# A one-token decoder block in float32: the ring of load buffers moved to a multiple of 256 bytes, and two late weight loads each cut in two

## The chip, the cores and the metric

The kernel runs on one core of a Trainium2 chip. The metric is the device time of one execution in microseconds (us), the median of several runs. The profile and the trace are those of one further execution, whose span is the time between the first and the last recorded instruction.

## The reference

One decode step of a block with adaptive layer norm, two batch rows, everything in float32. Attention looks at the last W = 4096 of 32768 cached positions.

```python
# B=2, D=512, HQ=32 query heads, HKV=8 key/value heads, DH=128, F=1792
mod = (silu(c) @ w_mod).reshape(2, 6, 1, 512)          # sa, ca, ga, sb, cb, gb
h = layernorm(x) * (1 + ca) + sa
q = (h @ wq) split into 32 heads
p = softmax(q . k_cache[:, :, -4096:] * 128**-0.5)      # 4 query heads share one k/v head
x = x + ga * ((p @ v_cache[:, :, -4096:]) @ wo)
h = layernorm(x) * (1 + cb) + sb
x = x + gb * (silu(h @ w1) @ w2)                        # w1 512x1792, w2 1792x512
```

## The kernel before

All of the large inputs come from device memory through one queue, SyncE's, into one ring: the pool `ring` of RING = 8 buffers, each 4096 floats (16,384 bytes) on each of 128 partitions. 45 loads stand in the queue in the order of the program and take the ring's buffers in turn: `w_mod` in four (`wm`), `wq` in four, then for each of 16 pairs t of key/value head and batch row one load of keys (`load_k`) and one of values (`load_v`), `wo` in four (`wo0`, `wo8`, `wo16`, `wo24`), `w1` in two (`w1_0`, `w1_2`), `w2` in four (`w2_0`, `w2_8`, `w2_11`, `w2_13`). The last ten are made by `load_runs`; the number in a name is the first row per partition that the load holds. A load may start when its ring buffer has been released by the engine that read what stood in it last, and when the load eight before it has landed. Some loads of a few kilobytes (`c_ch`, `x_ch`, `x_sp`) go to the pool `consts`, and so does every small constant that is built on the chip.

What one partition reads in one piece differs: 12,288 bytes of `w_mod`, 16,384 of `wq`, of the keys and of `wo`, four pieces of 4,096 for the values, 14,336 for each half of `w1`.

Work on a pair t: VectorE transposes the keys block by block (L341), TensorE multiplies them with the queries (L359), maximum and exponent follow on VectorE, TensorE and ScalarE, and TensorE weighs the values of the pair before (L303). After the last pair comes a tail in which each step needs the one before it:

- `acc_o` and `ao` (L475, L484): the attention output times `wo`, eight rows per partition from each of the four loads.
- layer norm: `x1T`, `mean_b`, `hT_b` on VectorE and TensorE.
- `hid` (L516): `hT_b` times `w1` in four steps k = 0..3; k = 0, 1 read `w1_0`, k = 2, 3 read `w1_2`. Between k = 1 and k = 2 stands the small product `var_b` (L525).
- `hidT`, `z`, `sgh`, `uT` (L533 to L545): transpose and SiLU on VectorE and ScalarE.
- `acc_yw` (L549): `uT` times the first eight rows per partition of `w2` (all in `w2_0`), tt = 0..7; then `acc_y` (L559) for tt = 8..13, with `gather` (L462) bringing `acc_yw` in after tt = 10.
- `yo` (L569, L570) and the store of the output (L572), also in SyncE's queue.

No scheduler reorders this: each engine runs its instructions in the order in which the program writes them. A matmul of the program is two records in the trace.

The pools are laid out in each partition one after the other in the order in which the function opens them. In the kernel before `consts` is opened first, and the ring begins at byte 49,088 of each partition, which is 192 above a multiple of 256. All eight buffers, 16,384 bytes apart, begin 192 above a multiple of 256.

Of the kernel before, what the change touches and what calls it, by code (L numbers as in the profile page):

```python
# [8 lines left out]
F32 = mybir.dt.float32  # L9
# [4 lines left out]
P = 128  # L14
# [5 lines left out]
RING = 8  # L20
# [3 lines left out]
def adaln_block(  # L24
# [24 lines left out]
    SCALE = DH**-0.5  # L49
    assert W == 4096  # L50

    consts = ctx.enter_context(tc.tile_pool(name="consts", bufs=1))
    ring = ctx.enter_context(tc.tile_pool(name="ring", bufs=RING))
    ktp = ctx.enter_context(tc.tile_pool(name="ktp", bufs=2))
    work = ctx.enter_context(tc.tile_pool(name="work", bufs=2))
    once = ctx.enter_context(tc.tile_pool(name="once", bufs=1))
# [3 lines left out]
    def const(shape, name):  # L60
        return consts.tile(shape, F32, name=name)

    def bank(tag, name):
        return (psum1 if tag in "CO" else psum).tile([P, 512], F32, tag=tag, name=name)

    def stream(name):
        return ring.tile([P, 4096], F32, tag="st", name=name)
# [20 lines left out]
    def load_runs(name, w, per, lo, hi):  # L88

        e = w.shape[1]  # L90
        t = stream(f"{name}{lo}")[:, : (hi - lo) * e].rearrange("p (q e) -> p q e", e=e)
        nc.sync.dma_start(t, w.rearrange("(p q) e -> p q e", q=per)[:, lo:hi, :])
        return t
# [19 lines left out]
    ident = const([P, P], "ident")  # L113
    make_identity(nc, ident)

    id4 = const([P, 32], "id4")
    nc.vector.tensor_reduce(
        id4, ident.rearrange("p (a r) -> p r a", r=32), axis=AX.X, op=ALU.add
    )
# [300 lines left out]
    ax = once.tile([P, P], F32, tag="ax", name="ax")  # L420
    for q0 in range(0, 32, 8):
        wot.append(load_runs("wo", wo, 32, q0, q0 + 8))
    w1t = [load_runs("w1_", w1, 4, k, k + 2) for k in (0, 2)]
    T2, WIDE = F // P, 8
    w2t = {}
    for lo, hi in ((0, WIDE), (WIDE, 11), (11, 13), (13, T2)):
        wt = load_runs("w2_", w2, T2, lo, hi)
        for tt in range(lo, hi):
            w2t[tt] = wt[:, tt - lo, :]
# [43 lines left out]
    for q in range(24):  # L473
        g = q % 4
# [37 lines left out]
    FC = F // 4  # L512
    hp = bank("A", "hid")[:, :FC]
    for k in range(4):
        for g in range(4):
            nc.tensor.matmul(  # L516
                hp[32 * g : 32 * g + 32, :],
                hT[:, k, :],
                w1t[k // 2][:, k % 2, g * FC : (g + 1) * FC],
                start=(k == 0),  # L520
                stop=(k == 3),
            )
        if k == 1:
            var = bank("B", "var_b")
            nc.tensor.matmul(var[:, :B], mean512, vs, start=True, stop=True)  # L525
            std = once.tile([P, B], F32, tag="stdb", name="std_b")
            nc.scalar.activation(std, var[:, :B], AF.Sqrt, bias=eps_t)
            rstd = once.tile([P, B], F32, tag="rstdb", name="rstd_b")
            nc.vector.reciprocal(rstd, std)
# [17 lines left out]
    for tt in range(WIDE):  # L547
        g = tt % 4
# [51 lines left out]
```

## Time and profile before

| what | value |
|---|---|
| median of 3 runs | 245.63 us (245.63 to 245.86) |
| the profiled execution | 245.34 us |
| its span | 243.1 us |
| TensorE busy | 154.8 us (64%) |
| VectorE busy | 102.4 us (42%) |
| ScalarE busy | 34.9 us (14%) |
| moved by DMA | 97.82 MB in 13467 packets |
| mean granted TensorE clock | 0.823 |

A busy share is an average over the whole span. Which engine or transfer sets the end is read from the chain that ended last and from the waits in each stage. The profiled execution took 2.24 us more than its span, which is what lies around the first and the last recorded instruction.

### The profile page before, as it was taken

To read this page: it belongs to the slowest core of one execution; us is meant where nothing else is said; L and a number is where in the kernel's file an instruction comes from. 1 tells how busy PE (TensorE), PEld (TensorE's weight loads), DVE (VectorE), ACT (ScalarE), POOL (GpSimd) and SP (SyncE) were. 2 spreads that over 40 slices of the span, in tenths; PEclk is the share of its full clock that TensorE was granted. 3 is DMA by queue.
4 is the path that set the end of the run, shared out by engine and by line. 5 is a ranking of instruction groups with operands and counts; after the bars stand their busy time and mean duration, and the time that the engine had idled before them with its cause. 6 is when DMAs were issued, how large, how long until landed. Compare 5 with 4: busy or idle time off the path is not lost.

```text
span 243.1 us, 4593 instructions
## 1 busy us (share of the span) xinstructions
PE 154.8 (64%) x2040; PEld 82.7 (34%) x2040; DVE 102.4 (42%) x179; ACT 34.9 (14%) x96; POOL 7.4 (3%) x27
## 2 busy tenths in 40 slices
PE   0294656067786596692963948487396488864854
PEld 0221001023453463451642625255163256103213
DVE  0604003772754835726457263563736721002030
ACT  2300000103320211220102112021111202003200
POOL 8000000000000000000000000000000000000000
PEclk9999579655997978897699789679869979779577
DMA  7999999999999999999999999999999999999970
GB/s 257 422 434 431 431 426 426 408 431 401 427 421 405 433 400 426 421 406 434 399 429 419 404 432 402 431 415 408 431 404 419 403 431 429 426 428 429 420 295 1
DMA packets 13467, 97.82 MB, mean 402 GB/s; under 512 B 888, under 2 KB 904, under 8 KB 9480
## 3 DMA queue, kind: packets, MB, share of 16 engines
q1 hardware_dynamic: 13448, 97.54, 97.0%
q8 instruction: 16, 0.26, 0.4%
q14 instruction: 3, 0.02, 0.0%
HBM read 97.53 MB, written 0.00 MB: 401 GB/s over the span
## 4 chain that ended last, share of the span: by engine, by line
DMA 67%; DVE 16%; PE 14%; SPq 1%; issue 1%; ACT 0%; POOL 0%; DVEq 0%; POOLq 0%
DMA k<-in_A_k_cache_dram 38%; DMA w<-in_B_w_dram 14%; DVE kT L341 12%; DMA wq<-in_A_wq_dram 12%; PE s L359 8%; DMA c_ch<-in_c_dram 2%; PE hid L516 1%; PE acc_yw L549 1%; PE o L303 1%; PE acc_y L559 1%; DVE qT L270 1%; SPq L71 1%; PE q L261 0%; DVE qbd L284 0%; DVE mx L367 0%
## 5 line engine op out<-in xcount | busy, mean ns | idle before, releaser
L359 PE MATMUL s<-kT,qbd 128*32 128x256 f32 x512 | 48.2, 532 | 49.0 <-DVE kT L341 49.0
L341 DVE STREAM_TRANSPOSE kT<-k 128x1024 f32<-128x1024 f32 x64 | 73.9, 1207 | 9.4 <-DMA k<-in_A_k_cache_dram 9.4
L303 PE MATMUL o<-v,ptb 128*32 128x128 f32 x1024 | 45.5, 297 | 0.0
L359 PEld LDWEIGHTS s<-kT,qbd 128*32 128x32 f32 x512 | 19.6, 145 | 70.0 <-DVE kT L341 53.4
L303 PEld LDWEIGHTS o<-v,ptb 128*32 128x32 f32 x1024 | 36.0, 119 | 5.6 <-issue 3.1
L367 DVE TENSOR_REDUCE mx<-s 128x1 f32<-128x256 f32 x16 | 6.8, 425 | 48.3 <-PE s L359 48.3
L391 ACT COPY bias<-bp 128x1 f32<-128x1 f32 x16 | 2.6, 160 | 123.2 <-PE bp L389 123.2
L261 PE MATMUL q<-wq,hq_T 128*32 128x512 f32 x64 | 11.7, 869 | 9.7 <-DMA wq<-in_A_wq_dram 9.7
L393 ACT ACTIVATE pr<-s,bias 128x256 f32<-128x256 f32 x16 | 11.8, 741 | 0.5
L475 PE MATMUL acc_o<-wo,oTn 128*32 128x512 f32 x48 | 8.6, 851 | 3.4 <-DMA wo<-in_A_wo_dram 3.1
L270 DVE STREAM_TRANSPOSE qT<-q 128x512 f32<-128x512 f32 x2 | 1.4, 717 | 19.1 <-PE q L261 18.8
L261 PEld LDWEIGHTS q<-wq,hq_T 128*32 128x32 f32 x64 | 2.2, 137 | 19.2 <-DMA wq<-in_A_wq_dram 11.1
L369 PE MATMUL mT<-ident,mx 128*1 128x128 f32 x32 | 7.3, 316 | 1.1 <-DVE mx L367 1.1
L375 DVE TENSOR_REDUCE mg<-mT 1x4 f32<-1x64 f32 x16 | 3.4, 210 | 10.5 <-PE mT L369 10.5
L406 PE MATMUL pT<-ident,pr 128*128 128x128 f32 x32 | 7.0, 300 | 0.4
L516 PE MATMUL hid<-w,hT_b 128*32 128x448 f32 x32 | 5.8, 868 | 1.8 <-DMA w<-in_B_w_dram 1.2
L494 DVE STREAM_TRANSPOSE aoT<-ao 128x128 f32<-128x128 f32 x1 | 0.3, 317 | 15.4 <-PE ao L484 15.4
L389 PEld LDWEIGHTS bp<-negscale,mrow 1*128 1x128 f32 x32 | 4.9, 190 | 5.6 <-DVE mrow L381 4.8
L409 ACT COPY ptb<-pT 128x256 f32<-128x256 f32 x16 | 6.0, 372 | 5.4 <-PE pT L406 5.3
L317 PE MATMUL o_all<-ob,selh 128*32 128x128 f32 x32 | 6.5, 284 | 0.4 <-ACT ob L312 0.4
L389 PE MATMUL bp<-negscale,mrow 1*128 1x1 f32 x32 | 6.2, 262 | 0.7 <-DVE mrow L381 0.2
L193 PE MATMUL mean_a<-mv_a,avg 128*128 128x1 f32 x2 | 0.6, 363 | 8.8 <-DVE mv_a L190 8.8
(123 smaller groups left out, 88.6 us busy)
## 6 DMA issues: line engine op xcount, KB each, us to landing
k<-in_A_k_cache_dram SPq DMA_DIRECT2D x16, 2048.0 KB, 32.0
v<-in_A_v_cache_dram SPq DMA_DIRECT2D x16, 2048.0 KB, 27.7
wq<-in_A_wq_dram SPq DMA_DIRECT2D x4, 2048.0 KB
wo<-in_A_wo_dram SPq DMA_DIRECT2D x4, 2048.0 KB, 27.9
wm<-in_w_mod_dram SPq DMA_DIRECT2D x4, 1536.0 KB, 8.6
w<-in_B_w_dram SPq DMA_DIRECT2D x2, 1792.0 KB
w<-in_B_w_dram SPq DMA_DIRECT2D x1, 2048.0 KB
w<-in_B_w_dram SPq DMA_DIRECT2D x1, 768.0 KB
```

What stands on the lines that cost most here:

```text
L261: nc.tensor.matmul(q_ps[n][32 * g : 32 * g + 32, :], hq_T[:, k, :], wv[:, n, g], start=(k == 0), stop=(k == 3),)
L303: nc.tensor.matmul(o_ps[32 * i : 32 * i + 32, :], pt[:, n % 2, o : o + 32], vt[:, i, n, :], start=(n == 0), stop=(n == 7),)
L317: nc.tensor.matmul(o_all[:, b, :], selh[:, HQ - G - G * h : 2 * HQ - G - G * h], weighted.o_sb, start=(t == 0), stop=(t == NP - 1), skip_g ...
L341: nc.vector.transpose(kT[t][:, n4].rearrange("p n j r -> p (n j r)"), kt[t][:, n4 * 1024 : (n4 + 1) * 1024],)
L359: nc.tensor.matmul(s_ps[32 * cc : 32 * cc + 32, :], qbd[h // 4][:, h % 4, b, j, :], kT[t][:, :, 2 * cc : 2 * cc + 2, j, :], start=(j == 0) ...
L367: nc.vector.tensor_reduce(mx, s_ps, axis=AX.X, op=ALU.max)
L369: nc.tensor.matmul(mT[0:1, :P], mx, ident, start=True, stop=True)
L389: nc.tensor.matmul(bp[:, 0:1], m, negscale, start=True, stop=True)
L393: nc.scalar.activation(pr.rearrange("p s k n -> p n s k"), s_ps.rearrange("p (n s k) -> p n s k", n=4, s=2), AF.Exp, bias=bias, scale=SCAL ...
L406: nc.tensor.transpose(tp[:, s * P : (s + 1) * P], pr[:, s].rearrange("p k n -> p (k n)"), ident)
L475: nc.tensor.matmul(acc[32 * g : 32 * g + 32, :], oTn[:, q, :], wot[q // 8][:, q % 8, :], start=(q < 4), stop=(q >= 20),)
L516: nc.tensor.matmul(hp[32 * g : 32 * g + 32, :], hT[:, k, :], w1t[k // 2][:, k % 2, g * FC : (g + 1) * FC], start=(k == 0), stop=(k == 3),)
```

## The change

The function opens a new pool `head` first, which holds the constant `id4` (128 bytes), and then the ring, before `consts`. With `id4` in front the ring begins at byte 16,640, which is 65 times 256. `consts` lies behind the ring and has the same size less `id4`. The loads of `w1` become three (`w1_0` as before, then one row per partition each in `w1_2` and `w1_3`, 7,168 bytes a piece), and the first eight rows of `w2` come in two loads of four (`w2_0`, `w2_4`, 8,192 bytes a piece).

```diff
+    head = ctx.enter_context(tc.tile_pool(name="head", bufs=1))
+    id4 = head.tile([P, 32], F32, name="id4")
+    ring = ctx.enter_context(tc.tile_pool(name="ring", bufs=RING))
     consts = ctx.enter_context(tc.tile_pool(name="consts", bufs=1))
-    ring = ctx.enter_context(tc.tile_pool(name="ring", bufs=RING))
...
-    id4 = const([P, 32], "id4")
...
-    w1t = [load_runs("w1_", w1, 4, k, k + 2) for k in (0, 2)]
+    w1t = []
+    for lo, hi in ((0, 2), (2, 3), (3, 4)):
+        wt = load_runs("w1_", w1, 4, lo, hi)
+        w1t.extend(wt[:, k, :] for k in range(hi - lo))
...
-    for lo, hi in ((0, WIDE), (WIDE, 11), (11, 13), (13, T2)):
+    for lo, hi in ((0, 4), (4, WIDE), (WIDE, 11), (11, 13), (13, T2)):
...
-                w1t[k // 2][:, k % 2, g * FC : (g + 1) * FC],
+                w1t[k][:, g * FC : (g + 1) * FC],
```

SyncE's queue at its end, from the first load of `w1` on. The shapes are partitions by floats; behind a row stand the semaphores it waits for, `DMAHW` for the landing of an earlier load, PE or DVE for the engine that releases the ring buffer. Before:

```order
L92 DMA w1_0_1570<-in_B_w1_dram 128x3584 [waits DMAHW1_49,PE_49]
L92 DMA w1_2_1572<-in_B_w1_dram 128x3584 [waits DMAHW2_49,DVE_49]
L92 DMA w2_0_1574<-in_B_w2_dram 128x4096 [waits DMAHW3_49,PE_49]
L92 DMA w2_8_1576<-in_B_w2_dram 128x1536 [waits DMAHW4_49,PE_49]
L92 DMA w2_11_1578<-in_B_w2_dram 128x1024 [waits DMAHW5_49,PE_49]
L92 DMA w2_13_1580<-in_B_w2_dram 128x512 [waits DMAHW6_49,PE_49]
L572 DMA out_0_dram<-yo_1754 4x2x128 [waits DMAHW7_49,DVE_49]
```

The same place in the queue after the change:

```order
L95 DMA w1_0_1573<-in_B_w1_dram 128x3584 [waits DMAHW1_49,PE_49]
L95 DMA w1_2_1575<-in_B_w1_dram 128x1792 [waits DMAHW2_49,DVE_49]
L95 DMA w1_3_1577<-in_B_w1_dram 128x1792 [waits DMAHW3_49,PE_49]
L95 DMA w2_0_1579<-in_B_w2_dram 128x2048 [waits DMAHW4_49,PE_49]
L95 DMA w2_4_1581<-in_B_w2_dram 128x2048 [waits DMAHW5_49,PE_49]
L95 DMA w2_8_1583<-in_B_w2_dram 128x1536 [waits DMAHW6_49,PE_49]
L95 DMA w2_11_1585<-in_B_w2_dram 128x1024 [waits DMAHW7_49,PE_49]
L95 DMA w2_13_1587<-in_B_w2_dram 128x512 [waits DMAHW0_49,PE_49]
L577 DMA out_0_dram<-yo_1761 4x2x128 [waits DMAHW1_49,DVE_49]
```

Two loads more, and each load from `w1_3` on takes a later buffer of the ring and a later semaphore. Before, `w2_11` and `w2_13` took the buffers of `wo0` and `wo8`. Now `w2_4` and `w2_8` take those, and `w2_11` and `w2_13` take the buffers of `wo16` and `wo24`.

TensorE's queue in the tail, from the first product with `w1` on (a count behind a row is the number of matmuls in a line). Before:

```order
L516 MATMUL hid_1678<-w1_0_1570,hT_b_225 32x448 x8
L525 MATMUL var_b_1687<-vs_1676,mean512_126 128x2
L516 MATMUL hid_1678<-w1_2_1572,hT_b_225 32x448 x8
L549 MATMUL acc_yw_1714<-w2_0_1574,uT_226 32x512 x8
L559 MATMUL acc_y_1723<-w2_8_1576,uT_226 32x128 x12
```

And after the change:

```order
L521 MATMUL hid_1685<-w1_0_1573,hT_b_228 32x448 x8
L530 MATMUL var_b_1694<-vs_1683,mean512_129 128x2
L521 MATMUL hid_1685<-w1_2_1575,hT_b_228 32x448 x4
L521 MATMUL hid_1685<-w1_3_1577,hT_b_228 32x448 x4
L554 MATMUL acc_yw_1721<-w2_0_1579,uT_229 32x512 x4
L554 MATMUL acc_yw_1721<-w2_4_1581,uT_229 32x512 x4
L564 MATMUL acc_y_1730<-w2_8_1583,uT_229 32x128 x12
```

The matmuls are the same in the same order; what has moved is the place where TensorE waits for a load, which stands now ahead of k = 2, of k = 3, of tt = 0 and of tt = 4. On VectorE, ScalarE and GpSimd nothing is added, removed or moved.

## The prediction

> **What bounds the kernel now.** I read first the page: shares, the slices of the DMA, the queues, the chain.
>
> ```profile
> span 243.1 us, 4593 instructions
> DMA  7999999999999999999999999999999999999970
> GB/s 257 422 434 431 431 426 426 408 431 401 427 421 405 433 400 426 421 406 434 399 429 419 404 432 402 431 415 408 431 404 419 403 431 429 426 428 429 420 295 1
> q1 hardware_dynamic: 13448, 97.54, 97.0%
> DMA 67%; DVE 16%; PE 14%; SPq 1%; issue 1%; ACT 0%; POOL 0%; DVEq 0%; POOLq 0%
> ```
>
> The 16 DMA engines are at 9 in every slice from the second to the 38th, and the queue's packets fill 97.0% of their span. So the loads run without a hole for about 230 us, and no engine makes them wait. Only two things can move the time: how long the packets take, and what lies behind the last load that the compute waits for. For the second I read the chain in order of time, at its end.
>
> ```profile
> 195.15 33.79 DMA w<-in_B_w_dram
> 228.94 0.04 issue
> 228.98 3.26 PE hid L516 x16
> 232.24 0.02 issue
> ...
> 234.74 2.80 PE acc_yw L549 x16
> 237.53 1.28 PE acc_y L559 x24
> ...
> 240.25 0.29 DVE yo L570
> ```
>
> The chain waits for `w1_2`, which lands at 228.94, and from there nothing but compute stands in it up to `yo`. The timeline of TensorE shows the same place, and the table by stretches the clock that was granted there (its last three columns: PEclk, DMA share, GB/s).
>
> ```profile
> 224.71 2.59 PE L516 MATMUL hid<-w,hT_b 128*32 128x448 f32 x16 [0.62 <-DVE sq L509]
> 227.23 0.59 PE L525 MATMUL var_b<-vs,mean 128*128 128x2 f32 x2
> 228.98 3.22 PE L516 MATMUL hid<-w,hT_b 128*32 128x448 f32 x16 [1.16 <-DMA w<-in_B_w_dram]
> 237.24 1.58 PE L559 MATMUL acc_y<-w,uT 128*32 128x128 f32 x24
> 238.95 0.92 PE L559 MATMUL acc_y<-w,uT 128*32 128x128 f32 x24
> 224.60:227.30 2.70, 2.59 (x17) 0.68 (x17) 0.16 (x1) 0.00 (x0) 0.00 (x0) 0.65 1.03 431
> 228.90:232.30 3.40, 3.22 (x16) 0.60 (x16) 0.03 (x1) 0.52 (x1) 0.00 (x0) 0.51 0.99 417
> ```
>
> TensorE sits idle 1.16 us before the second half of `hid`, and then works 3.2 us at half the clock on both its steps k = 2 and k = 3.
>
> **What a packet costs.** A ring at another offset can only change the packets, so I took their mean times from the DMA view in four windows: 18:42 (almost all pieces of 16,384 bytes), 50:200 (keys and values), 6.1:6.3 (the small loads) and 10:16 (`w_mod`), in this order.
>
> ```profile
> DMA packets 705, 10.32 MB, mean 430 GB/s; under 512 B 75, under 2 KB 75, under 8 KB 75
> q1 hardware_dynamic: 704, 10.31, 100.8%
> DMA packets 10204, 62.61 MB, mean 417 GB/s; under 512 B 477, under 2 KB 477, under 8 KB 8350
> q1 hardware_dynamic: 10190, 62.40, 101.2%
> DMA packets 88, 0.11 MB, mean 531 GB/s; under 512 B 80, under 2 KB 80, under 8 KB 80
> q1 hardware_dynamic: 88, 0.11, 151.7%
> DMA packets 237, 2.58 MB, mean 430 GB/s; under 512 B 27, under 2 KB 27, under 8 KB 27
> q1 hardware_dynamic: 237, 2.58, 101.0%
> ```
>
> (A share slightly over 100% means that neighbouring packets overlap, or belong to the window by their start.) In 10:16: 1.010 x 16 x 6 us = 96.96 us for 210 packets of 12,288 bytes and 27 small ones, some 460 ns for a large one. In 6.1:6.3: 1.517 x 16 x 0.2 = 4.85 us; less 8 x 0.46 leaves 1.17 us for 80 small packets, 14.6 ns each. In 18:42: 387.1 us, less 75 small ones, over 629 packets: 614 ns for 16,384 bytes. In 50:200: 2428.8 us, less 477 x 14.6 ns and 1840 x 614 ns, over 7873 packets: 164 ns for 4,096 bytes. The line through the last two is 0.0366 ns a byte and 14.4 ns a packet beyond its bytes.
>
> **The change, part by part.**
>
> *The ring's offset.* It adds no instruction. It could take away at most what a packet costs beyond its bytes: 14.4 ns x (13448 - 888 small) / 16 = 785 packets per engine, 11.3 us; the other bound is 0, and I see no reason for a loss. Which is nearer? The packets to the unaligned ring pay 14.4 ns (by `w_mod`: 460 - 449.7 = 10 ns). The 64 pieces of 128 bytes of `c_ch` and `x_ch` go to columns 128 bytes apart in tiles 128 above a multiple of 256, so half of them begin at a multiple already. The 80 small packets hold 103 bytes in the mean, 3.8 ns by the line, so they pay 14.6 - 3.8 = 10.8 ns beyond their bytes. Half of them aligned, they cost no less than the large ones of `w_mod`, of which none is. So the cost looks like one that every packet has, and I take 0 us.
>
> The Trainium skill says otherwise, in DMA: Bandwidth & Descriptors, section How a descriptor splits into AXI transactions: what does not begin at a multiple of 256 bytes has its first transaction begin at the boundary below, and the bytes ahead of the start still cost time. It states this of reads, while the ring is written; no run here shows it yet. By it the sum would go down by the 5.3 us of the first rival.
>
> *`w1_2` in two.* 128 packets more up to its end, 8 per engine x 14.4 ns = 0.12 us: `w1_3` lands at 228.94 + 0.12 = 229.06. `w1_2` holds 0.918 MB now, and its successor needs 0.918 MB / 430 GB/s = 2.13 us, so it lands at 226.9. TensorE is in `var_b` until 227.23 + 0.59 = 227.82, so k = 2 starts then and not at 228.98. At the same clock k = 2 takes half of 3.26 us, to 229.45, by when `w1_3` has landed; k = 3 goes to 231.08. `hid` ends 232.24 - 231.08 = **1.16 us earlier**. Bounds: if k = 3 is held by its landing alone, 229.06 + 0.04 + 1.63 = 230.73, gain 1.51; at the clock of 224.60:227.30 (16 records in 2.59 us) 229.1 + 1.3 = 230.4 against 228.98 + 2.59 = 231.57 before, gain 1.2. If k = 2 started no earlier, nothing.
>
> *`w2_0` in two, and what is late next.* The landings at the end follow from the view of the issues (median us from issue to landing; one load each) and the timeline of SyncE:
>
> ```profile
> 209.90 0.33 SPq L92 DMA_DIRECT2D w<-in_B_w_dram  x1
> 213.10 0.33 SPq L92 DMA_DIRECT2D w<-in_B_w_dram  x1
> w<-in_B_w_dram SPq DMA_DIRECT2D x1, 512.0 KB, 27.1
> w<-in_B_w_dram SPq DMA_DIRECT2D x1, 256.0 KB, 24.5
> ```
>
> `w2_11` lands at 237.0, `w2_13` at 237.6. Counting back at 430 GB/s: `w2_8` 237.0 - 1.22 = 235.8, `w2_0` 234.0. With 16 more packets per engine (0.23 us) the new landings are 234.2 (`w2_4`), 236.0 (`w2_8`), 237.2 and 237.8, and `w2_0` about 231.8. They are needed, 1.16 us earlier than now: tt = 0 at 234.74 - 1.16 = 233.58 (landed at 231.8); tt = 4 some 0.9 to 1.4 us after that, 234.5 or later (234.2); `acc_y` at 237.24 - 1.16 = 236.08 (236.0); tt = 11 at 237.8 (237.2); tt = 13 some 0.5 later, 238.3 (237.8). Each is in time, `w2_8` by 0.1. Uncut, `w2_0` would land at 234.1 and hold tt = 0 for 0.5 us; so the second cut is what keeps 0.5 of the 1.16.
>
> *The added waits.* `w1_3` takes the buffer that `w2_0` had, `w2_0` that of `w2_8`, `w2_4` and `w2_8` those of `w2_11` and `w2_13`: issued at 209.90 and 213.10. Only `w2_11` and `w2_13` wait for something new, TensorE's last matmuls from `wo16` and `wo24`:
>
> ```profile
> 215.43 3.46 PE L475 MATMUL acc_o<-wo,oTn 128*32 128x512 f32 x16 [2.39 <-DMA wo<-in_A_wo_dram]
> 221.43 1.06 PE L484 MATMUL ao<-wo,oTn 128*32 128x128 f32 x32
> ```
>
> They are issued at 218.9 and 222.5, 9 us later than now. Behind them stands only the store of the output at 240.57. Their cover is the bytes still ahead of them in the queue: their packets' turn comes at 236.0 and 237.2, 15 us after the issue. Cost 0. Two more issues cost SyncE 0.33 us each in time in which it waits anyway.
>
> **Sum.** The span goes from 243.1 to 241.94 us. The profiled execution took 245.34 us, 2.24 more than its span, and the median is 245.63; the same 1.16 off it gives **244.5 us**.
>
> **Rivals.**
>
> *The offset pays after all.* A transfer that must also pass the 192 bytes below its start costs 192 x 0.0366 = 7.0 ns a packet. Of the 785 packets per engine 32 belong to `w2`, the others stand ahead of `w1_3`'s landing: 753 x 7.0 = 5.3 us, 239.2 us with the first gain. For it: the 14.4 ns leave room for it. Against it: the small packets above. Anything between is possible, such as half of it, 241.8 us. The page named above is the one whose rule this is.
>
> *The cut buys nothing.* If the landings are later than I counted back (`w2_8` has 0.1 us to spare, the last two 0.5), or TensorE loses the time to a lower clock, the gain falls below 0.5 us: 245.1 to 246.
>
> *Each added load costs the queue a pause.* A pause p per load moves `w2_13` to 237.8 + 2p. It is needed by 239.45 for the end that the kernel has now (238.3 + 1.16), so from p = 0.8 us the change is slower. With p = 2 it lands at 241.8, 2.4 us too late: 248.0 us. Against it: `w2_13` lands 0.6 us after `w2_11`, and 256 KB at 430 GB/s take 0.61, which leaves no pause. The Trainium skill speaks for it, in SBUF — State Buffer, section The DMA setup-cost knee: each transfer pays about 2 us whatever its size. The trace disagrees for loads that queue up behind each other, by those 0.6 us.
>
> **How the numbers follow.** About 0.2% (0.5 us) is what a measurement of this kernel can tell from no change. The forecast, 244.0 to 245.0, has 0.62; the offset paying (below 244.0) 0.18; the cut buying nothing 0.14; slower, by the pause or otherwise, 0.06. That is 0.80 for faster, 0.14 for the same, 0.06 for slower. The range, 240.5 to 245.6 us, leaves out the offset's larger effects (0.09) and about half of the last two cases (0.10).
>
> **What would show it.** Right: the chain ends over `hid` from a landing at about 229.1, with the first eight records of its second half starting near 227.8 and all ended near 231.1; tt = 0 of `acc_yw` near 233.6 without a wait for a load; the windows 18:42 and 50:200 with the same packet times, 614 and 164 ns. The first rival shows as about 607 and 157 ns there, and as landings of `wo` that come up to 5 us earlier. I am wrong if `acc_y` waits for `w2_8` or `w2_11` by more than 0.3 us, if `w2_13` sets the end, or if GB/s in the slices of the loop rises.

## The result and the profile after

The changed kernel takes 241.72 us (median of 4 runs, 240.72 to 242.15) against 245.63 us. The ratio is 0.9836 with a 95% interval of 0.9803 to 0.9868: 3.9 us less, where 1.16 us were forecast. The time lies in the stated range, the direction was right, and the larger part of the gain came from the term that the prediction had put at zero.

The page of the changed kernel: span, slices of the DMA, the queue of the loads (packets, MB, share of 16 engines), the chain by engine.

```profile
span 240.0 us, 4597 instructions
DMA  6999999999999999999999999999999999999970
GB/s 242 429 434 429 437 426 426 419 440 406 444 417 412 436 412 438 427 411 439 404 440 426 410 438 417 427 426 418 438 414 423 416 436 431 431 430 414 426 309 3
q1 hardware_dynamic: 13736, 97.54, 97.0%
DMA 65%; PE 17%; DVE 15%; SPq 1%; issue 1%; ACT 0%; DVEq 0%
```

There are 288 packets more, the same bytes and the same share, in a span that is 3.1 us shorter. (The ring takes 52 loads instead of 50; the 45 given above for the kernel before is a miscount of 4 + 4 + 32 + 4 + 2 + 4.) The DMA is still busy in every slice from the second to the 38th. So each byte has become cheaper. The DMA view for the windows 18:42 and 50:200 (two rows each):

```profile
DMA packets 703, 10.31 MB, mean 429 GB/s; under 512 B 74, under 2 KB 74, under 8 KB 74
q1 hardware_dynamic: 702, 10.29, 100.2%
DMA packets 10273, 63.76 MB, mean 425 GB/s; under 512 B 488, under 2 KB 488, under 8 KB 8345
q1 hardware_dynamic: 10259, 63.54, 101.3%
```

By the prediction's working: 384.8 us less 74 small packets over 628 large ones, 611 ns for 16,384 bytes (614 before); 2431.2 us less 488 x 14.6 ns and 1914 x 611 ns over 7857 packets, 160 ns for 4,096 bytes (164 before). In the loop the core receives 425 GB/s instead of 417.

What that does to the tail is read at `wo24`, the last load of `wo`. First the row of the kernel before, then TensorE's timeline of the changed kernel, one row of its table by stretches (PEclk is the third number from the end), and the last load that stands in its chain.

```profile
220.32 1.08 PE L484 MATMUL ao<-wo,oTn 128*32 128x128 f32 x32 [1.43 <-DMA wo<-in_A_wo_dram]
```

```profile
217.51 1.76 PE L489 MATMUL ao<-wo,oTn 128*32 128x128 f32 x32 [2.91 <-DMA wo<-in_A_wo_dram]
219.45 1.90 PE L489 MATMUL ao<-wo,oTn 128*32 128x128 f32 x32
223.42 2.12 PE L521 MATMUL hid<-w,hT_b 128*32 128x448 f32 x16 [0.46 <-DVE hT_b L512]
225.47 0.59 PE L530 MATMUL var_b<-vs,mean 128*128 128x2 f32 x2
225.98 2.68 PE L521 MATMUL hid<-w,hT_b 128*32 128x448 f32 x16
231.21 3.50 PE L554 MATMUL acc_yw<-w,uT 128*32 128x512 f32 x16 [2.55 <-DVE uT L550]
217.50:221.40 3.90, 3.84 (x72) 3.44 (x72) 0.00 (x0) 0.00 (x0) 0.00 (x0) 0.56 0.97 409
187.63 29.84 DMA wo<-in_A_wo_dram
```

`wo24` lands 2.8 us earlier. From there on the chain consists of compute alone: no matmul with `w1` or `w2` waits for a load. In this execution that is so because TensorE had 0.56 of its clock in `ao` (3.9 us for the stretch that took 2.2 us before) and reached k = 2 only at 225.98.

### The profile page after: what moved, and what is told of

It is laid out like the page before. It is cut to its first block, busy times and chain, and to the rows that moved or that the text cites. A ratio compares the mean times of both kernels' runs of the same rounds, so it can differ in the third digit from the quotient of the medians.

```text
span 240.0 us, 4597 instructions
## 1 busy us (share of the span) xinstructions
PE 153.6 (64%) x2040; PEld 84.4 (35%) x2040; DVE 102.5 (43%) x179; ACT 34.9 (15%) x96; POOL 7.4 (3%) x27
## 4 chain that ended last, share of the span: by engine, by line
DMA 65%; PE 17%; DVE 15%; SPq 1%; issue 1%; ACT 0%; DVEq 0%
DMA k<-in_A_k_cache_dram 38%; DMA wo<-in_A_wo_dram 12%; DMA wq<-in_A_wq_dram 12%; DVE kT L343 11%; PE s L361 7%; DMA c_ch<-in_c_dram 2%; PE hid L521 2%; PE o L305 2%; PE q L263 2%; PE acc_yw L554 1%; PE ao L489 1%; PE acc_y L564 1%; SPq L74 1%; PE mT L371 1%; DVE qbd L286 0%
## 5 line engine op out<-in xcount | busy, mean ns | idle before, releaser
L361 PE MATMUL s<-kT,qbd 128*32 128x256 f32 x512 | 46.8, 519 | 46.6 <-DVE kT L343 46.6
L305 PEld LDWEIGHTS o<-v,ptb 128*32 128x32 f32 x1024 | 37.0, 121 | 5.9 <-issue 3.9
L263 PE MATMUL q<-wq,hq_T 128*32 128x512 f32 x64 | 12.8, 940 | 10.2 <-DMA wq<-in_A_wq_dram 10.2
L480 PE MATMUL acc_o<-wo,oTn 128*32 128x512 f32 x48 | 7.0, 723 | 3.3 <-DMA wo<-in_A_wo_dram 2.9
L227 PE MATMUL m_sp<-wm,scT 128*32 128x512 f32 x32 | 5.7, 796 | 0.0
```

The lines of the kernel that those rows point to most:

```text
L263: nc.tensor.matmul(q_ps[n][32 * g : 32 * g + 32, :], hq_T[:, k, :], wv[:, n, g], start=(k == 0), stop=(k == 3),)
L305: nc.tensor.matmul(o_ps[32 * i : 32 * i + 32, :], pt[:, n % 2, o : o + 32], vt[:, i, n, :], start=(n == 0), stop=(n == 7),)
L361: nc.tensor.matmul(s_ps[32 * cc : 32 * cc + 32, :], qbd[h // 4][:, h % 4, b, j, :], kT[t][:, :, 2 * cc : 2 * cc + 2, j, :], start=(j == 0) ...
L480: nc.tensor.matmul(acc[32 * g : 32 * g + 32, :], oTn[:, q, :], wot[q // 8][:, q % 8, :], start=(q < 4), stop=(q >= 20),)
```

## The experiments

Packet times below are worked out as above, from the windows 18:42 and 50:200 of each profile. The column wo24 has the time at which `ao` starts on what `wo24` brought (in e11 on its second piece). Each ratio is to the kernel before as it ran beside that run: 245.00 us beside e1 to e4, 245.11 beside e5 to e8, 244.91 beside e9 to e11.

| run | ring above a multiple of 256 | cuts | ratio to the kernel before (95%) | 16,384 / 4,096 bytes, ns | wo24, us |
|---|---|---|---|---|---|
| before | 192 | none | 1 | 614 / 164 | 220.3 |
| e1 | 0 | none | 0.9887 (0.9863 to 0.9912) | 612 / 159 | 217.4 |
| e2 | 192 | w1, w2 | 1.0002 (0.9982 to 1.0023) | 615 / 164 | 220.4 |
| e3 | 192, ring first | w1, w2 | 0.9973 (0.9956 to 0.9989) | 615 / 164 | 220.5 |
| e4 (changed) | 0 | w1, w2 | 0.9831 (0.9806 to 0.9856) | 611 / 159 | 217.5 |
| e5 | 128 | w1, w2 | 0.9976 (0.9955 to 0.9996) | 614 / 164 | 220.6 |
| e6 | 64 | w1, w2 | 0.9987 (0.9969 to 1.0006) | 615 / 164 | 220.7 |
| e7 | 32 | w1, w2 | 0.9988 (0.9970 to 1.0006) | 615 / 164 | 221.0 |
| e8 | 0, source 64 | w1, w2 | 0.9850 (0.9820 to 0.9881) | 611 / 159 | 217.6 |
| e9 | 0 | w1 | 0.9888 (0.9861 to 0.9914) | 611 / 159 | 217.2 |
| e10 | 0 | w2 | 0.9870 (0.9838 to 0.9901) | 611 / 159 | 217.4 |
| e11 | 0 | wo, w1, w2 | 0.9844 (0.9819 to 0.9869) | 611 / 160 | 217.9 |

**Which part makes the gain: the offset alone (e1), the cuts alone (e2).** e1 is the changed kernel with the two lists of loads as they were:

```diff
-    for lo, hi in ((0, 2), (2, 3), (3, 4)):
+    for lo, hi in ((0, 2), (2, 4)):
...
-    for lo, hi in ((0, 4), (4, WIDE), (WIDE, 11), (11, 13), (13, T2)):
+    for lo, hi in ((0, WIDE), (WIDE, 11), (11, 13), (13, T2)):
```

> The ring at a multiple of 256 bytes, the loads of w1 and w2 uncut as in the kernel before. Theory A (the offset shortens the packets): 50:200 gives 160 ns for 4,096 bytes and 18:42 gives 611 ns for 16,384, as in the changed kernel; wo's last load lands near 217.5 instead of 220.3; the chain then stands again on the second half of w1, so the time is 2.8 us below the kernel before, 242.8 us. Theory B (the cuts make the gain, the offset is worth 0): 164 and 614 ns, 245.6 us.

It took 242.37 us beside 245.00 us of the kernel before. The ratio of 0.9887 is 2.8 us, as theory A said. TensorE's timeline of e1:

```profile
217.43 1.93 PE L489 MATMUL ao<-wo,oTn 128*32 128x128 f32 x32 [1.72 <-DMA wo<-in_A_wo_dram]
226.18 2.02 PE L521 MATMUL hid<-w,hT_b 128*32 128x448 f32 x16
231.14 3.64 PE L554 MATMUL acc_yw<-w,uT 128*32 128x512 f32 x16 [2.94 <-DMA w<-in_B_w_dram]
```

`wo24` lands 2.9 us earlier than before with no cut at all. The expected wait for the second half of `w1` is not there; the wait is for `w2`'s uncut first load, before `acc_yw`.

e2 is the changed kernel with the pools in the old order:

```diff
-    head = ctx.enter_context(tc.tile_pool(name="head", bufs=1))
-    id4 = head.tile([P, 32], F32, name="id4")
-    ring = ctx.enter_context(tc.tile_pool(name="ring", bufs=RING))
     consts = ctx.enter_context(tc.tile_pool(name="consts", bufs=1))
+    ring = ctx.enter_context(tc.tile_pool(name="ring", bufs=RING))
...
+    id4 = const([P, 32], "id4")
```

> The cuts alone, the ring at 192 above a multiple of 256 as before. Theory A: 164 and 614 ns; only the prediction's term of the cuts is left, hid ends 1.16 us earlier: 244.5 us. Theory B: 241.7 us, the changed kernel's time. A third: the cuts are worth nothing by themselves, 245.6 us.

The packets are those of theory A (615 and 164 ns), the time is that of the third: 1.0002, so by its interval the cuts by themselves are worth at most 0.4 us, where the prediction had 1.16. Its timeline, and its clock between 217 and 222 us:

```profile
220.44 1.94 PE L488 MATMUL ao<-wo,oTn 128*32 128x128 f32 x32 [2.22 <-DMA wo<-in_A_wo_dram]
229.13 2.22 PE L520 MATMUL hid<-w,hT_b 128*32 128x448 f32 x16
217.00:222.00 5.00, 2.78 (x40) 1.45 (x36) 0.00 (x0) 1.87 (x2) 0.00 (x0) 0.50 0.99 418
```

Here TensorE had half its clock in `ao`, came to k = 2 at 229.13 and found `w1` there. The 1.16 us of waiting that the cut was to fill do not exist in such an execution.

**Offset or place (e3).** The changed kernel with a wider tile ahead of the ring, so that the ring still comes first in memory:

```diff
-    id4 = head.tile([P, 32], F32, name="id4")
+    id4 = head.tile([P, 80], F32, name="id4")[:, 0:32]
```

> The changed kernel with the pool ahead of the ring 192 bytes larger: the ring still stands ahead of the constants, but begins 192 above a multiple of 256 again. Theory A (it is the offset): packets as in the kernel before, 164 and 614 ns, and 244.5 us as with the cuts alone. Theory C (it is where the ring and the constants lie, not the offset): 160 and 611 ns, 241.7 us.

The DMA view of 50:200 and TensorE's timeline:

```profile
DMA packets 10206, 62.63 MB, mean 418 GB/s; under 512 B 477, under 2 KB 477, under 8 KB 8351
q1 hardware_dynamic: 10192, 62.42, 101.2%
220.54 1.26 PE L489 MATMUL ao<-wo,oTn 128*32 128x128 f32 x32 [2.98 <-DMA wo<-in_A_wo_dram]
229.19 0.96 PE L521 MATMUL hid<-w,hT_b 128*32 128x448 f32 x8 [0.30 <-DMA w<-in_B_w_dram]
234.18 1.07 PE L554 MATMUL acc_yw<-w,uT 128*32 128x512 f32 x8 [0.42 <-DMA w<-in_B_w_dram]
236.14 0.86 PE L564 MATMUL acc_y<-w,uT 128*32 128x128 f32 x24 [0.90 <-DMA w<-in_B_w_dram]
```

The packets and the landing are those of the kernel before, so theory C falls: with nothing but 192 bytes more ahead of the ring, 3.0 us of landing are lost. At 0.9973 the cuts and the order of the pools show here as 0.7 us together. This execution had the full clock from 226 us on (1.00 in 226:232 and in 232:238). `hid` then waits for `w1_3`, `acc_yw` for `w2_4` and `acc_y` for `w2_8`. Less the 0.04 us between a landing and the matmul, they land at 229.15, 234.14 and 236.10, where the prediction's list had 229.06, 234.2 and 236.0.

> The changed kernel itself, beside the others on the same chip: 241.7 us by every theory (240.7 to 242.2 so far), 160 and 611 ns.

The changed kernel, run beside these three, came to 240.67 us, 0.9831. In this profile it had the full clock in `ao` and waits for `w1_3`, whose landing is 3.1 us earlier than e3's:

```profile
217.47 1.08 PE L489 MATMUL ao<-wo,oTn 128*32 128x128 f32 x32 [1.50 <-DMA wo<-in_A_wo_dram]
226.06 0.96 PE L521 MATMUL hid<-w,hT_b 128*32 128x448 f32 x8 [1.18 <-DMA w<-in_B_w_dram]
```

**Which offsets cost (e5, e6, e7).** The same edit as e3 with `P, 64` (128 bytes), `P, 48` (64 bytes) and `P, 40` (32 bytes).

> The changed kernel with the ring 128 above a multiple of 256. Packet times from 50:200 and 18:42 were 160 and 611 ns at a multiple of 256, 164 and 614 at 192 above. Theory P (the cost grows with the offset): 162 to 163 and 613 ns, 242.8 us. Theory Q (any start off a multiple of 256 costs the same): 164 and 614 ns, 244.3 us. Theory R (a multiple of 128 is enough): 160 and 611 ns, 241 us.

> The ring 64 above a multiple of 256. Theory P (grows with the offset): 161 and 612 ns, 242 us. Theory Q (all the same): 164 and 614 ns, 244.3 us. If instead the distance up to the next multiple of 256 counts (192 here, 64 at an offset of 192), it is the worst of all, above 166 ns and 245 us.

> The ring 32 above a multiple of 256. Theory P: 160 to 161 and 611 to 612 ns, 241.5 us. Theory Q: 164 and 614 ns, 244.3 us. If a start off a multiple of 64 costs more than the others, more than 164 ns and later than 245 us.

Theory Q held for all three: 163.9, 163.9 and 163.8 ns for 4,096 bytes, 614 to 615 for 16,384. The cost does not grow with the offset, and a multiple of 128 is not enough. The rows of 50:200, e5 and then e6:

```profile
DMA packets 10209, 62.64 MB, mean 418 GB/s; under 512 B 477, under 2 KB 477, under 8 KB 8354
q1 hardware_dynamic: 10195, 62.43, 101.2%
DMA packets 10209, 62.63 MB, mean 418 GB/s; under 512 B 477, under 2 KB 477, under 8 KB 8355
q1 hardware_dynamic: 10195, 62.42, 101.2%
```

**The read side (e8).** Keys and values are read from 48 floats ahead, the ring stays at a multiple of 256:

```diff
+    def early(cache, b, h):
+        at = (SK - W) * DH - 48
+        return cache[b, h].rearrange("s d -> (s d)")[at : at + W * DH]
...
-            t, k_cache[b, h, SK - W :, :].rearrange("(p n) d -> p (n d)", p=P)
+            t, early(k_cache, b, h).rearrange("(p e) -> p e", p=P)
...
-            t, v_cache[b, h, SK - W :, :].rearrange("(i p n) d -> p i (n d)", i=4, p=P)
+            t, early(v_cache, b, h).rearrange("(i p e) -> p i e", i=4, p=P)
```

> The changed kernel, ring at a multiple of 256, but every key and value load reads from 192 bytes ahead of where it should, so that each piece in device memory begins 64 above a multiple of 256 (its attention is over shifted data). Theory S (only the written side counts): 160 ns as in the changed kernel, 241 us. Theory T (the read side costs as the written one does): 4 ns on each of 640 packets per engine of the keys and values, 2.6 us, 243.5 us. By the rule that reads begin at the boundary below (Trainium skill, DMA: Bandwidth & Descriptors, section How a descriptor splits into AXI transactions) an estimate is 64 bytes more a packet, 64 x 0.0366 = 2.3 ns, 162 ns and 1.5 us: 242.2 us.

Theory S held. The rows of 50:200 and the landing of `wo24`:

```profile
DMA packets 10269, 63.74 MB, mean 425 GB/s; under 512 B 486, under 2 KB 486, under 8 KB 8342
q1 hardware_dynamic: 10255, 63.52, 101.2%
217.63 1.93 PE L493 MATMUL ao<-wo,oTn 128*32 128x128 f32 x32 [2.13 <-DMA wo<-in_A_wo_dram]
```

159 ns for the values and 0.9850. The window 18:42 holds `wq`, whose reads were not moved, so the 16,384 bytes of the keys are read from the trace's packet records: 1651 of the 1671 between 50 and 180 us took 611 ns (1662 of 1671 in the changed kernel, none of 1664 in the kernel before). Where the reads begin in device memory does not show, where the writes begin in the core's memory does. That the caches themselves begin at a multiple of 256 in device memory is taken for granted here; no run shows it. What is shown is that two starts 192 bytes apart cost the same.

**One cut at a time (e9, e10).** The ring at a multiple of 256, and one of the two lists of e1's diff.

> Ring at a multiple of 256, only w1's second half cut, w2's first eight rows in one load as before. With no cut 242.4 us were measured, with both 240.7 to 241.7. Theory U (both cuts are needed, as the prediction says): w2's first load lands near 231.1 and holds tt = 0 of acc_yw, where the changed kernel starts it at 229.6 with the full clock: 241.9 us. Theory V (the cut of w1 does it all): 241 us.

> Ring at a multiple of 256, only w2's first eight rows cut, w1's second half in one load as before. Theory U: hid ends as late as without cuts where the clock is full (landing 226.1 and 2 us of matmuls), tt = 0 comes no earlier than 231: 242 us. Theory W (the cut of w2 does it all, because its one load set the start of acc_yw): 241 us.

0.9888 and 0.9870: by their intervals neither can be told from e1 without cuts (0.9887). e9's six runs took 241.66 to 242.77 us, all more than theory V's 241, and its interval lies just above that of the changed kernel in e4 (0.9806 to 0.9856), so theory V falls. e10 can't be told from the changed kernel either, so theory W stands. The start of `hid`'s second half in e9 and in e10, in this order, and then the clock of both between 217 and 222 us:

```profile
225.85 2.41 PE L521 MATMUL hid<-w,hT_b 128*32 128x448 f32 x16
225.99 3.21 PE L521 MATMUL hid<-w,hT_b 128*32 128x448 f32 x16 [1.47 <-DMA w<-in_B_w_dram]
217.00:222.00 5.00, 3.76 (x72) 3.25 (x72) 0.95 (x6) 0.00 (x0) 0.00 (x0) 0.65 0.99 415
217.00:222.00 5.00, 2.78 (x78) 2.39 (x82) 1.63 (x10) 1.15 (x1) 0.00 (x0) 1.00 1.00 422
```

e9's execution came to k = 2 late and its cut had nothing to do; e10's came early, without the cut, and waited 1.47 us. The two profiles differ in the clock that TensorE was granted in `ao`, 0.65 and 1.00, and so do the two profiles of the changed kernel, which is one and the same program (0.66 and 1.00 in 217:222). Theory U's times, 241.9 and 242, are near the medians of 241.91 and 241.58; for the cut of `w2` the runs do not settle it.

**One cut more (e11).** `wo24` in two loads as well:

```diff
-    for q0 in range(0, 32, 8):
-        wot.append(load_runs("wo", wo, 32, q0, q0 + 8))
+    for lo, hi in ((0, 8), (8, 16), (16, 24), (24, 28), (28, 32)):
+        wt = load_runs("wo", wo, 32, lo, hi)
+        wot.extend(wt[:, q, :] for q in range(hi - lo))
```

> The changed kernel with wo's last load cut in two as well (rows 24 to 27 and 28 to 31). Half of ao's matmuls and the gather then run before the last landing near 217.5, so ao ends 1.1 us earlier at full clock and 2.1 at half. If the end hangs on that landing, as in the changed kernel's first profile, 240.2 us; if w1's last load at 226.1 holds it anyway, as in its second profile, 241 us, no gain.

240.96 us, 0.9844: the second of the two cases, no gain over the changed kernel that can be told from noise (0.9831 in e4). Its timeline shows why:

```profile
217.87 1.08 PE L490 MATMUL ao<-wo,oTn 128*32 128x128 f32 x32 [1.15 <-DMA wo<-in_A_wo_dram]
226.43 0.96 PE L522 MATMUL hid<-w,hT_b 128*32 128x448 f32 x8 [0.42 <-DMA w<-in_B_w_dram]
231.37 1.54 PE L555 MATMUL acc_yw<-w,uT 128*32 128x512 f32 x8 [0.39 <-DMA w<-in_B_w_dram]
233.31 1.51 PE L565 MATMUL acc_y<-w,uT 128*32 128x128 f32 x24 [0.40 <-DMA w<-in_B_w_dram]
```

`ao` is through earlier, and then `hid`, the second half of `acc_yw` and `acc_y` each wait for a load. In this execution the tail goes at the pace of the DMA, and earlier compute ends in those waits.

## Why the prediction was right in direction and wrong in its parts

**The bound.** Right. The loads fill the span, and what shortened them shortened the kernel: 2.9 us earlier at `wo24`, 2.8 us less time (e1).

**The offset.** This is the step that failed: the cost of the offset was put at 0 us, and it was 2.8 us (e1). "I take 0 us" came from setting 10.8 ns, which the small packets cost beyond their bytes, against the 10 ns of `w_mod`'s large ones. Both sides of that comparison were at fault.

`w_mod`'s packets do cost the same at either offset. The changed kernel's window 10:16 shows it:

```profile
DMA packets 240, 2.61 MB, mean 434 GB/s; under 512 B 28, under 2 KB 28, under 8 KB 28
q1 hardware_dynamic: 240, 2.61, 101.9%
```

97.8 us less 28 small packets over 212 give 460 ns, as before. But they were the wrong packets to ask, because the cost sets in only later, in the same ring at the same offset. The packet records of the kernel before show it as the share of packets that took no longer than is usual with the ring at a multiple of 256 (460 ns for 12,288 bytes, 611 for 16,384): 0.98 in 10:14, all `w_mod`; then, in packets of 16,384 bytes, 0.85 in 18:22, 0.31 in 28:36 and 0.08 in 38:46. In the changed kernel the share is 0.94, 1.00, 0.99 and 1.00.

And the small packets cost less than the prediction took them to. By the packet records of the window 6.1:6.3 the pieces of 128 bytes took 13 ns and those of 4 bytes 9 ns, 12 in the mean and not 14.6; beyond their bytes that is some 8 ns. The line through keys and values had 14.4 ns (9.3 with the ring at a multiple of 256), so 6 ns a packet were passed over, and of them the prediction's own working shows 14.4 - 10.8 = 3.6.

What the offset costs is summed directly from the packet records. Up to `wo24`, 8192 packets of 4,096 bytes took 163.7 ns in the mean before and 159.6 after the change, and 3072 of 16,384 bytes 616.2 and 612.1. Over 16 engines that is 2.9 us, and `wo24` landed 2.8 to 2.9 us earlier. That 3.6 ns times 785 packets give 2.8 us too is partly luck, because the 10.8 was off.

**The first rival** had the effect right, at about half its price, and the mechanism wrong. It charged 7.0 ns a packet for passing the 192 bytes below its start. Measured are 3 to 4.5 ns, the same at 32, 64 and 128 bytes, so passing the bytes below the start is not the mechanism. Its signs were to be about 607 and 157 ns and landings of `wo` up to 5 us earlier; seen are 611 and 160 ns and 2.8 us. GB/s in the loop rose from 417 to 425, which the prediction had named as a sign of being wrong. The rule of the Trainium skill (DMA: Bandwidth & Descriptors, section How a descriptor splits into AXI transactions) is about reads; for a read that begins 64 above a multiple of 256 e8 shows no such cost. Its boundary, 256 bytes, is the one that the written side has here.

**The cut of `w1`.** The mechanism was right where its condition holds, the condition was not seen. The 1.16 us were read from one execution in which TensorE had 0.84 to 0.93 of its clock between 217 and 226 us:

```profile
217.00:222.00 5.00, 3.57 (x75) 1.88 (x71) 0.00 (x0) 1.87 (x2) 0.00 (x0) 0.84 1.00 426
222.00:226.00 4.00, 2.16 (x34) 1.13 (x27) 1.63 (x10) 0.00 (x0) 0.00 (x0) 0.93 1.00 418
```

With half the clock in `ao` (e2) the wait is gone. That is the second rival, "the cut buys nothing", which named a lower clock as one of its reasons. At an offset of 192 the cuts measured 0.0 us (e2) and, with the other order of the pools, 0.7 us (e3). At 0, from e1's 0.9887 to e4's 0.9831, they are worth 1.4 us, to within some 0.9. The term should have been a range from 0 to 1.2 us; how often an execution has which clock was not measured. Whether the cuts are worth more at one offset than at the other stays open.

**The late landings.** The list was right to within 0.1 us in e3, but not the times at which TensorE would need them. There `acc_y` waited 0.90 us for `w2_8`, where the prediction gave it 0.1 us to spare and named more than 0.3 as a sign of error, because TensorE, at full clock, came some 0.8 us earlier than reckoned. In the changed kernel's two profiles no matmul with `w2` sits idle for a load.

**The added waits** cost nothing, as forecast. `w2_13` is issued at 221.41, and nothing waits for it:

```profile
221.41 0.33 SPq L95 DMA_DIRECT2D w<-in_B_w_dram  x1
```

**The pause per load** fell: the cuts alone are not slower (1.0002), and the three-way cut of e11 is as fast as the changed kernel. The Trainium skill's rule that each transfer pays about 2 us (SBUF — State Buffer, section The DMA setup-cost knee) does not show here in loads that queue up behind each other.

**The sum** of 1.16 us thus left out 2.8 us and counted on up to 1.2 us that a given execution may not have. The measured 3.9 us are e1's 2.8 and 1.1 more, but that the rest comes so near to 1.16 confirms nothing, at an uncertainty of 0.9. The time missed the forecast of 244.0 to 245.0, which had a chance of 0.62, and fell where the offset pays, which had 0.18. That it lies in the range at all is due to the rival with the larger gain, which was carried in it; that its half price, 241.8 us, agrees with the 241.72 is partly luck, since half was named as an example and the mechanism is another.

## What to carry to other kernels

In a kernel that its loads bound, look where the buffers that the DMA writes begin, and start them at a multiple of 256 bytes: here one small constant ahead of the ring was worth 1.1%, for no instruction. When two estimates of a cost per packet differ by a few ns, multiply the difference by the number of packets before calling them equal. Compare such costs only between packets of the same stage: here the first loads to the ring did not show what the later ones paid. A wait in the tail of one execution is worth its length only if the next execution has it too: check the granted clock in front of it.

## What the runs showed of the hardware

- A write that begins 32, 64, 128 or 192 bytes above a multiple of 256 cost 3 to 4.5 ns more per packet in the mean, for 4,096 and for 16,384 bytes alike. In the trace's packet records it is a spread and not a constant: of the 8320 packets of 4,096 bytes 8295 took 159 ns in the changed kernel, but 1973 in the kernel before, where all but 22 of the others took 160 to 172.
- The cost is not there from the start. `w_mod`'s packets of 12,288 bytes, written first, showed none of it (460 ns at both offsets). In the kernel before it set in while `wq` was loaded, whose share of packets at 611 ns or less fell from 0.85 in 18:22 to 0.31 in 28:36. What sets it in, and what in the chip makes the spread, the runs do not tell. The pieces of 128 bytes took 13 ns in nearly all cases (a few 11), but they came before that time and go to `consts`, so they show nothing for or against.
- Reads from device memory that begin 192 bytes earlier than in the changed kernel, 64 above a multiple of 256 if the tensors begin at one, cost the same: 159 ns for 4,096 bytes and 611 for 16,384.
- The granted clock of one program differs from execution to execution: 0.66 and 1.00 between 217 and 222 us in the changed kernel's two profiles.
